# Gate logits of the first chunk on POOL and ACT, wider feature instructions, other homes for the key masks, an uneven last tile and a seeded planner, in a fused attention and feed-forward kernel

## The chip, the cores and the metric

One core of one Trainium2 chip runs the whole program. The metric is device time in microseconds (us), the median of several executions; lower is better. Single executions of one kernel here mostly lie within 0.3% of each other. The chip names five engines: TensorE (PE), VectorE (DVE), ScalarE (ACT), GpSimd (POOL) and SyncE (SP, used to issue DMAs).

## The reference, cut to what matters

The input x is 2048 tokens by 512 features, bf16. A per-token gate `g` mixes an attention branch `a` and a gated feed-forward branch `b`:

```python
g = sigmoid((x * gate_w).sum(-1, keepdims=True))     # one number per token
a = A_ref(x, wq, wk, wv, wo, beta)                   # 32 heads of 16, four segments ("chunks") of 512 tokens
b = B_ref(x, W_gate, W_up, W_down)                   # relu(x Wg) * (x Wu), then W_down
return g * a + (1 - g) * b
# A_ref, per chunk: softmax attention inside the chunk, mixed with a memory
#   a_mem = phi(q) M / (phi(q) z + 1e-6);  phi(t) = t + 1 if t > 0 else exp(t)
#   M and z are then updated with phi(k) and v of this chunk
```

Of the kernel before, what the change touches and what calls it, by code (L numbers as in the profile page):

```python
# [1 line left out]

# [53 lines left out]
class Op:  # L56
    __slots__ = ("engs", "eng", "fns", "occs", "lat", "reads", "writes", "name", "dma", "nbytes", "mode", "ep", "role",
                 "after", "preds", "stream", "idx", "start", "end", "done", "cidx", "gate")

    def __init__(self, alts, reads=(), writes=(), name="", lat=0.0, dma=False, nbytes=0, mode="f", ep=None, role=None):  # L60
# [15 lines left out]
        self.gate = None  # L76
        self.stream = self.idx = self.start = self.end = None
# [9 lines left out]
class Sched:  # L87
# [3 lines left out]
    def __init__(self, ndma=16, nbanks=4):  # L91
# [11 lines left out]
        self.dma_end = {}  # L103
        self.dma_busy = 0.0
# [131 lines left out]
    def _waits(self, e, deps):  # L236
        for st, idx in sorted(deps.items(), key=lambda kv: (kv[0] == e, kv[0])):
            if idx <= 0 or self.know[e][st] >= idx:
                continue
            self.prog[e].append(("wait", st, 16 * idx if st.startswith("dma") else idx))  # L240
            kn = self.know[e]
            for k2, v2 in self.snap[st][idx].items():
                if v2 > kn[k2]:
                    kn[k2] = v2
            kn[st] = max(kn[st], idx)

    def place(self, op, e, start):
# [18 lines left out]
        if op.dma:  # L266
# [4 lines left out]
            self.cnt[st] += 1  # L271
            inc = 16
# [20 lines left out]

    def _choose(self, e):
# [17 lines left out]
        if rdy:  # L312
            best = min(rdy, key=lambda h: (h[0], h[1]))
# [26 lines left out]
    def emit(self, block):  # L340
        sec = {"pe": block.tensor, "act": block.scalar, "dve": block.vector, "pool": block.gpsimd, "sp": block.sync}
        for e in self.ENGS:
            def body(engobj, prog=self.prog[e], e=e):
                for item in prog:
                    if item[0] == "wait":
                        engobj.wait_ge(self.sem[item[1]], item[2])
                    else:
                        _, op, st, inc = item
                        op.fns[e](engobj).then_inc(self.sem[st], inc)
# [3 lines left out]
def plan(S, D, F):  # L353
# [11 lines left out]
        ("gwc", [128, KT], BF16), ("braw", [128, 32], BF16), ("eb", [128, 32], F32), ("romgh", [128, 32], F32), ("epsv", [128, 32], F32),  # L365
        ("gexp", [128, NT], F32), ("omg", [128, NT], F32), ("gexpT", [128, NT * 4], F32), ("c2g", [128, 2, 4, 32], F32), ("gwb", [128, 512], BF16), ("gl", [128, NT], F32),
        ("rden", [128, 32], F32), ("rdg", [128, 32], F32), ("rdm", [128, 128], F32), ("pm8", [128, 8], F32), ("pm", [128, 2], F32), ("ident", [128, 128], BF16), ("g4", [4, 128], BF16),
# [3 lines left out]
def build_kernel(nc, A_x, A_wq, A_wk, A_wv, A_wo, A_beta, W_g, W_u, W_d, gate_w, out):  # L371
# [5 lines left out]
    sc = Sched()  # L377
# [14 lines left out]
def program(sc, nc, T, PL, PA, A_x, A_wq, A_wk, A_wv, A_wo, A_beta, W_g, W_u, W_d, gate_w, out, NSEG, KT, NF, NT, EPS, SCALE):  # L392
# [34 lines left out]
    for i, eng in enumerate(("sp", "act", "sp", "act")):  # L427
# [4 lines left out]
    load("act", ["g4"], V.g4[:], gate_w.rearrange("(kt p) -> kt p", p=128), 1 << 12)  # L432
# [17 lines left out]
    load("sp", ["gwb"], V.gwb[:], gate_w.partition_broadcast(128), 1 << 17)  # L450
# [58 lines left out]
    xps.append(warm(8, 128, 1, 0))  # L509
# [13 lines left out]
    ep_w = Epoch()  # L523
    gw_pe = pe(lambda e: e.matmul(A(ep_w)[:, 0:KT], lhsT=V.g4[:, :], rhs=V.ident[0:KT, 0:KT], start=True, stop=True), 60, reads=["g4", "ident"], name="gwT", ep=ep_w, role="w")
    gw_act = act(lambda e: e.activation(V.gwc[:], A(ep_w)[:, 0:KT], ACT.Copy), 180, writes=["gwc"], name="gwc", ep=ep_w, role="r")
    gw_pe.after = 9000.0
    gexpT_r = {}
    gq = {"pe": [], "act": [], "dve": [], "flex": [], "sp": []}
    for c in range(NSEG):
        t0, t1 = 4 * c, 4 * c + 4  # L530
        gx = V.gexp[:, t0:t1]
        if c == 0:
            ep_g = Epoch()

            def f_gmm(e):
                for t in range(4):
                    for kt in range(KT):
                        ins = e.matmul(A(ep_g)[:, t:t + 1], lhsT=V.xT[:, kt, t * 128:(t + 1) * 128], rhs=V.gwc[:, kt:kt + 1], start=(kt == 0), stop=(kt == KT - 1))
                return ins
            gq["pe"].append(pe(f_gmm, 4 * KT * 26.0, reads=xt(0) + ["gwc"], name="gmm", ep=ep_g, role="w"))  # L540
            gq["act"].append(act(lambda e, gx=gx: e.activation(gx, A(ep_g)[:, 0:4], ACT.Exp), 190, writes=[f"gexp{c}"], name="gexp", ep=ep_g, role="r"))
        else:
# [6 lines left out]
            gq["act"].append(act(lambda e, t0=t0, t1=t1, gx=gx: e.activation(gx, V.gl[:, t0:t1], ACT.Exp), 215, reads=[f"gl{t}" for t in range(t0, t1)], writes=[f"gexp{c}"], name="gexp"))  # L549
# [4 lines left out]
        for a in range(4):  # L554
            for jj in range(4):
                dst = V.gexpT[32 * jj:32 * jj + 32, :].rearrange("q (t a) -> q t a", a=4)[:, t0:t1, a]
# [367 lines left out]
```

## The kernel before: what the change and the argument touch

The kernel is not written as a fixed stream. It lists operations with their reads, writes and an estimated cost. A planner places them: on each engine it always takes, from the heads of several queues with priorities, the operation that its own cost estimates say is ready. The result is one fixed instruction order for each engine, with semaphore waits. So **a change of one operation or one estimate can reorder everything after it**, and the hardware then runs that order strictly, engine by engine.

```python
    def _choose(self, e):                      # pick the next operation of engine e
        ...
        rdy = [h for h in heads if h[1] <= now + 20.0]
        if rdy:
            best = min(rdy, key=lambda h: (h[0], h[1]))    # priority, then ready time
            return best[2], best[1]
        ...
```

Gate of chunk 0 on PE, the rest on DVE, then 16 small copies per chunk that spread the gate over partitions:

```python
gw_pe = pe(... matmul of gate_w and an identity ..., name="gwT")        # gate_w into a column
gw_act = act(... V.gwc <- PSUM ...)
if c == 0:
    def f_gmm(e):                              # 16 one-column matmuls
        for t in range(4):
            for kt in range(KT):
                ins = e.matmul(A(ep_g)[:, t:t + 1], lhsT=V.xT[:, kt, ...], rhs=V.gwc[:, kt:kt + 1], ...)
    gq["act"].append(act(... V.gexp <- exp(PSUM) ...))
...                                            # other chunks: DVE multiplies and sums
for a in range(4):                             # "gate copies": 32x4 elements each
    for jj in range(4):
        gq["flex"].append(... ("dve", tensor_copy, 150), ("act", Copy, 215) ..., name="gexpT")
```

Masked keys, the feature map phi in halves of 512 columns, and a score "quad": four row-tiled matmuls into one PSUM area, whose exp on ACT (1.88 us each, 80 of them) must end before the next quad may write there.

```python
km = lambda e: e.tensor_scalar(V.kp[:, ks, :], V.kT[:, G, :], V.pm[:, p:p + 1], None, ALU.mult)
alts = [("dve", km, 390)] + ([("pool", km, 680)] if s else [])
...
acts.append(act(... V.phiq[:, G, :] <- exp(qT) ..., name=f"qexp{s}_{G}"))
sbs.append(dve(... V.ttmp <- max(qT, 0) + 1 ..., name=f"qts{s}_{G}"))
sbs.append(dve(... V.phiq <- min(V.phiq, V.ttmp) ..., name=f"qphi{s}_{G}"))
...
pes.append(pe(fq, ..., writes=[f"bankL{b}" for b in range(4)], name=f"quad{s}_{tag}", mode="r"))
acts.append(act(... V.E <- exp(SCALE * PL) ..., reads=bankL, name=f"exp{s}_{tag}"))
```

Small constants at the start: `eb = exp(beta)` on ACT, then `romgh = eb + 1` and `epsv = 1e-6 * romgh` on DVE. The last output tile is computed as two pieces of 256 columns, so that the final eviction and store are small.

The softmax here doesn't subtract the row's maximum and nothing guards it: scores larger than these inputs give would overflow.

## Time and profile before

| | before |
|---|---|
| time, median of 3 (later 6 with the pairing runs) | 273.62 us (273.89) |
| span of the profiled execution | 272.4 us |
| busy PE / DVE / ACT / POOL | 264.6 / 206.2 / 196.0 / 120.9 us |

The head of the profile page of the kernel before: busy time with its share of the span and the number of instructions, then PE's busy share in 40 slices of the span (9 is 90% or more).

```profile
PE 264.6 (97%) x2126; PEld 115.8 (43%) x2161; DVE 206.2 (76%) x411; ACT 196.0 (72%) x194; POOL 120.9 (44%) x168
...
PE   8999999999998999999999999999999999999996
```

PE is busy all the way but for the first and last slices and one in the middle. A busy PE is not yet a PE at its peak, because the ends of matmuls are modelled. So a second reading was made: the distance from the **start** of one matmul to the start of the next, for each pair of shapes. Its median is what I call the *spacing*. An excess over it is a *stall*. In this trace a 512-column matmul follows another after 216 ns, 128 columns after 59 ns; the Trainium skill ("TensorE: Matmul & The Clock Gate", section "Wait — 56ns, not 53.3ns?") gives N/2.4 GHz plus about 2.5 ns when warm, 215.7 ns for 512, and this trace agrees. For 128 columns the same formula gives 55.8 ns, and the trace has 59, 3 ns more. A full-array matmul before a score quad takes 312 ns, 96 more. The skill's "TensorEngine Tiling (Array Packing)", section "Key Properties", says that a change of tiling mode drains the engine. The drain itself is not seen in the trace, but the longer spacing fits it and puts a number to it.

Put to the whole order, the spacings explain the time up to the cold start and few stalls. The largest stall is told by the list of waits of PE (two of its lines; the first is the head of the program):

```profile
PE psL L492 <- PEq L909: 0.8, 1, 0.8
PE psA L652 <- DVE phiq L603: 0.8, 1, 0.8
```

L652 are the denominators of the memory read, L603 the last step of phi(q). The timeline just before shows what L603 stood behind on DVE (columns: start us, us, engine, line, operation, shapes):

```profile
83.14 0.69 DVE L781 TENSOR_SCALAR rl<-psA 128x512 bf16<-128x512 f32 x1 [0.32 <-PE psA L772]
83.86 2.11 DVE L557 COPY gexpT<-gexp 32x4 f32<-32x4 f32 x7
84.14 1.23 POOL L699 TENSOR_SCALAR_AFFINE_SELECT E<-E 128x512 bf16<-128x512 bf16 x2 [0.32 <-ACT E L696]
86.01 0.42 DVE L603 TENSOR_TENSOR phiq<-phiq,ttmp 128x512 bf16<-128x512 bf16 x1
```

and PE in the same stretch:

```profile
85.09 0.60 PE L811 MATMUL psA<-wd,hT 128*128 128x512 bf16 x2
86.49 0.59 PE L652 MATMUL psA<-Mbd,phiq 128*128 128x8 bf16 x16 [0.79 <-DVE phiq L603]
```

Seven gate copies of four columns each hold DVE for 2.11 us, and PE stands for 0.79 us by the profile, 0.93 us by the spacings. The planner had put 150 ns on such a copy; on DVE they took 240 ns on average. The groups (count, then busy us and mean ns, then idle time before) that the change bears on:

```profile
L608 POOL TENSOR_SCALAR kp<-kT,pm 128x512 bf16<-128x512 bf16 x16 | 27.3, 1708 | 1.4 <-PE psL L691 0.8 <-DVE kT L605 0.4
L608 DVE TENSOR_SCALAR kp<-kT,pm 128x512 bf16<-128x512 bf16 x16 | 6.8, 430 | 1.3 <-PE psL L691 1.3
L558 ACT ACTIVATE gexpT<-gexp 32x4 f32<-32x4 f32 x40 | 8.3, 206 | 1.0
L557 DVE COPY gexpT<-gexp 32x4 f32<-32x4 f32 x24 | 5.8, 240 | 0.7
L538 PE MATMUL psA<-gwc,xT 128*128 128x1 bf16 x16 | 0.6, 164 | 0.0
```

The masks on POOL (L608) were planned at 680 ns and took 1708. The start, where PE waits for neither of the first two quads (`eb` comes when the load of beta, `braw`, has landed):

```profile
10.68 0.23 ACT L514 ACTIVATE eb<-braw 128x32 f32<-128x32 bf16 x1 [4.42 <-DMA braw<-in_A_beta_dram]
13.55 0.40 PE L691 MATMUL psL<-qT,kp 32*128 32x512 bf16 x4
14.05 1.86 ACT L696 ACTIVATE E<-psL 128x2048 bf16<-128x2048 f32 x1
```

The end of the program, with the two 256-column pieces:

```profile
269.28 0.60 PE L804 MATMUL psA<-wo,oT 128*128 128x256 bf16 x4
269.92 0.47 ACT L821 ACTIVATE osb<-psA,omg 128x256 bf16<-128x256 f32 x1 [1.43 <-PE psA L804]
```

### The profile page before, as it was taken

The numbers are of one execution on the slowest core, as the hardware profiler recorded it, in microseconds if no ns is written. First come the engines' busy times: TensorE is split into PE (matmuls) and PEld (weight loads), VectorE is DVE, ScalarE is ACT, GpSimd is POOL, SyncE is SP. The second block draws the span as 40 slices with busy tenths as digits, with TensorE's granted clock in tenths as the row PEclk, the third lists the DMA queues.
The fourth block names the chain that finished last, engine by engine and source line by source line (L and its number), as shares of the span: only waits on it lengthen the run. The fifth ranks groups of instructions, "written<-read, shape, count | busy, mean of one in ns | idle before, by whom it ended". The sixth has DMA issues, their size and how long they took to land.

```text
span 272.4 us, 5341 instructions
## 1 busy us (share of the span) xinstructions
PE 264.6 (97%) x2126; PEld 115.8 (43%) x2161; DVE 206.2 (76%) x411; ACT 196.0 (72%) x194; POOL 120.9 (44%) x168
## 2 busy tenths in 40 slices
PE   8999999999998999999999999999999999999996
PEld 5444434443443443443435343434344343444445
DVE  4789999999999989998987958885956274957200
ACT  3279898898798778888878977977887676952122
POOL 5023397879495374934364743243433333320000
PEclk9999999999999999999999999999999999999999
DMA  7999934301200234100113110100120000000011
GB/s 231 272 361 207 282 60 92 45 23 39 59 2 1 61 77 99 39 22 0 23 21 76 41 58 22 40 1 0 22 45 17 28 30 23 0 2 0 0 41 39
DMA packets 31025, 17.01 MB, mean 62 GB/s; under 512 B 20760, under 2 KB 31000, under 8 KB 31000
## 3 DMA queue, kind: packets, MB, share of 16 engines
q1 hardware_dynamic: 30416, 16.14, 23.9%
q10 hardware_dynamic: 584, 0.53, 0.7%
q8 instruction: 17, 0.28, 0.4%
q14 instruction: 8, 0.07, 0.1%
HBM read 9.84 MB, written 2.10 MB: 44 GB/s over the span
## 4 chain that ended last, share of the span: by engine, by line
PE 92%; DVE 4%; issue 2%; DMA 1%; ACT 0%
PE psA L772 36%; PE psA L811 16%; PE psA L592 10%; PE psL L691 9%; PE psA L717 7%; PE psA L590 5%; PE psA L804 4%; DVE gexpT L557 1%; PE psA L665 1%; DMA hT<-in_A_x_dram 1%; PE psA L636 1%; PE psL L500 1%; PE psA L652 1%; DVE qT L599 0%; PE psL L492 0%
## 5 line engine op out<-in xcount | busy, mean ns | idle before, releaser
L696 ACT ACTIVATE E<-psL 128x2048 bf16<-128x2048 f32 x80 | 150.0, 1875 | 33.6 <-PE psL L691 32.4
L699 POOL TENSOR_SCALAR_AFFINE_SELECT E<-E 128x512 bf16<-128x512 bf16 x128 | 83.4, 671 | 116.6 <-ACT E L696 111.9
L772 PE MATMUL psA<-xT,wu 128*128 128x512 bf16 x216 | 58.5, 380 | 0.7 <-issue 0.3
L772 PE MATMUL psA<-xT,wg 128*128 128x512 bf16 x213 | 57.2, 380 | 1.1 <-issue 0.8
L811 PE MATMUL psA<-wd,hT 128*128 128x512 bf16 (+1 forms) x230 | 53.0, 367 | 0.8 <-issue 0.6
L783 DVE TENSOR_TENSOR hT<-psA,rl 128x512 bf16<-128x512 f32 x56 | 38.0, 680 | 10.5 <-PE psA L772 10.2
L811 PEld LDWEIGHTS psA<-wd,hT 128*128 128x128 bf16 x238 | 21.6, 98 | 24.0 <-issue 3.8
L691 PE MATMUL psL<-qT,kp 32*128 32x384 bf16 (+3 forms) x512 | 31.7, 301 | 0.0
L780 ACT ACTIVATE rl<-psA 128x512 bf16<-128x512 f32 x34 | 20.3, 597 | 15.2 <-PE psA L772 11.2
L772 PEld LDWEIGHTS psA<-xT,wg 128*128 128x128 bf16 x224 | 20.2, 98 | 25.0 <-issue 3.1
L772 PEld LDWEIGHTS psA<-xT,wu 128*128 128x128 bf16 x224 | 20.3, 98 | 24.8 <-issue 2.0
L608 POOL TENSOR_SCALAR kp<-kT,pm 128x512 bf16<-128x512 bf16 x16 | 27.3, 1708 | 1.4 <-PE psL L691 0.8
L722 DVE STREAM_TRANSPOSE Tn<-psA 128x512 f32<-128x512 f32 x32 | 21.0, 692 | 6.7 <-PE psA L717 6.7
L691 PEld LDWEIGHTS psL<-qT,kp 32*128 32x128 bf16 x512 | 8.9, 92 | 33.5 <-ACT E L696 15.7
L717 PE MATMUL psA<-E,vaug 128*17 128x256 bf16 (+3 forms) x512 | 20.2, 300 | 0.0
L820 DVE TENSOR_SCALAR osb<-psA,omg 128x512 bf16<-128x512 f32 x10 | 7.4, 744 | 14.1 <-PE psA L811 14.1
L781 DVE TENSOR_SCALAR rl<-psA 128x512 bf16<-128x512 f32 x22 | 15.1, 687 | 3.8 <-PE psA L772 3.5
L592 PE MATMUL psA<-xT,wq 128*128 128x512 bf16 x62 | 16.3, 384 | 0.2 <-issue 0.2
L804 PE MATMUL psA<-wo,oT 128*128 128x512 bf16 (+1 forms) x67 | 16.2, 366 | 0.2 <-DVE oTt L736 0.2
L592 PE MATMUL psA<-xT,wk 128*128 128x512 bf16 x60 | 15.8, 380 | 0.3 <-issue 0.2
L590 PE MATMUL psA<-wv,xT 128*128 128x512 bf16 x63 | 15.5, 380 | 0.1
L717 PEld LDWEIGHTS psA<-E,vaug 128*17 128x17 bf16 x512 | 10.7, 90 | 9.6 <-issue 2.7
(74 smaller groups left out, 236.9 us busy)
## 6 DMA issues: line engine op xcount, KB each, us to landing
out_dram<-osb SPq DMA_DIRECT2D x15, 128.0 KB, 1.7
wg<-in_B_W_gate_dram SPq DMA_DIRECT2D x8, 224.0 KB, 6.1
wu<-in_B_W_up_dram SPq DMA_DIRECT2D x8, 224.0 KB, 6.5
wd<-in_B_W_down_dram SPq DMA_DIRECT2D x1, 1792.0 KB
osb<-in_A_x_dram SPq DMA_DIRECT2D x12, 128.0 KB, 2.2
wk<-in_A_wk_dram SPq DMA_DIRECT2D x4, 128.0 KB, 4.0
wv<-in_A_wv_dram SPq DMA_DIRECT2D x4, 128.0 KB, 3.6
wo<-in_A_wo_dram SPq DMA_DIRECT2D x1, 512.0 KB, 5.4
```

Of the source, the lines that this page charges most:

```text
L590: ins = e.matmul(A(ep)[:, :], lhsT=V.xT[:, kt, tok + col * 128:tok + (col + 1) * 128], rhs=w[:, kt, :], start=(kt == 0), stop=(kt == KT - 1))
L592: ins = e.matmul(A(ep)[:, :], lhsT=w[:, kt, col * 128:(col + 1) * 128], rhs=V.xT[:, kt, tok:tok + 512], start=(kt == 0), stop=(kt == KT - 1))
L608: km = lambda e, G=G, p=p, ks=ks: e.tensor_scalar(V.kp[:, ks, :], V.kT[:, G, :], V.pm[:, p:p + 1], None, ALU.mult)
L691: ins = q.matmul(PL[:, jj, o:o + w], lhsT=V.kp[32 * jj:32 * jj + 32, kslot(s, n), 128 * j:128 * j + 128], rhs=V.qT[32 * jj:32 * jj + 32, q ...
L696: acts.append(act(lambda a, e=e: a.activation(V.E[:, e, :, :], PL[:, :, :], ACT.Exp, scale=SCALE), t_act(2048), reads=[f"bankL{b}" for b i ...
L699: pools.append(pool(lambda g, ap=ap: g.affine_select(out=ap, in_=ap, compare_op=ALU.is_ge, fill=0.0, base=0, pattern=[[0, 4], [1, 128]], c ...
L717: ins = q.matmul(A(ep)[32 * jj:32 * jj + 17, c:512], lhsT=V.vaug[:, s % 2, j, 8 * G + 2 * jj + p, :], rhs=V.E[:, e, jj, o:o + w], start=(j ...
L722: ds.append(dve(lambda e, p=p, ep=eps[p]: e.transpose(V.Tn[:, p, :], A(ep)[:, :]), t_dve(512), writes=[f"Tn{p}"], name=f"tr{s}_{G}_{p}", e ...
L772: ins = e.matmul(A(ep)[:, :], lhsT=w[:, kt, f * 128:(f + 1) * 128], rhs=V.xT[:, kt, c * 512:(c + 1) * 512], start=(kt == 0), stop=(kt == K ...
L783: evs.append(dve(lambda e, ep=eu, r=r, hs=hs: e.tensor_tensor(V.hT[:, hs, :], A(ep)[:, :], V.rl[:, r, :], ALU.mult), t_dve(512), reads=[f" ...
L804: ins = e.matmul(A(ep)[:, 0:c1 - c0], lhsT=V.oT[:, o0 + G, i * 128:(i + 1) * 128], rhs=V.wo[:, G, c0:c1], start=st_ and G == 0, stop=sp_ a ...
L811: ins = e.matmul(A(ep)[:, 0:c1 - c0], lhsT=V.hT[:, slots[f], i * 128:(i + 1) * 128], rhs=V.wd[:, f, c0:c1], start=st_ and f == f0, stop=sp ...
```

## The change

Its intent: take the gate of chunk 0 off PE, the bottleneck; halve the number of phi instructions; move the slow key masks off POOL; make the last eviction smaller; correct several of the planner's cost estimates; and let seeded random offsets of up to 400 ns decide among operations that are ready at equal priority, so that many orders can be tried.

```diff
     def _choose(self, e):
-            best = min(rdy, key=lambda h: (h[0], h[1]))
+            best = min(rdy, key=lambda h: (h[0], h[1] + self.jitter(h[2])))   # random() * 400 per operation, seed 59
@@ loads
-    load("act", ["g4"], V.g4[:], gate_w.rearrange("(kt p) -> kt p", p=128), 1 << 12)
+    load("act", ["gwb"], V.gwb[:], gate_w.partition_broadcast(128), 1 << 17)
-    load("sp", ["gwb"], V.gwb[:], gate_w.partition_broadcast(128), 1 << 17)          # was late, on SP
@@ gate of chunk 0 (gwT, gwc and the 16 gate matmuls removed)
+            for t in range(4):
+                gq["pool"].append(pool(... Tn[t % 2] <- hT[t] * gwb ..., 1250, name=f"gml{t}"))
+                gq["act"].append(act(... Copy of Tn[t % 2], accum_out=V.gl[:, t:t + 1] ..., name=f"gad{t}"))
@@ gate copies: contiguous destination, cost 150 -> 200 on DVE
@@ phi: for odd G, one instruction of 128x1024 for groups G-1 and G
-    alts = [("dve", km, 390)] + ([("pool", km, 680)] if s else [])
+    alts = [("dve", km, 420)] + ([("act", ka, 720)] if s else [])
@@ last tile
-    for c0, c1 in (((0, 512),) if t < NT - 1 else ((0, 256), (256, 512))):
+    for c0, c1 in (((0, 512),) if t < NT - 1 else ((0, 384), (384, 512))):
@@ one warm-up matmul fewer; estimates of three DVE operations raised; the first x tiles swap queues
```

More of the change, by code (lines that the diff above doesn't have):

```diff
@@ L1 @@
 import contextlib
+import random
 import numpy as np
@@ L57 @@
     __slots__ = ("engs", "eng", "fns", "occs", "lat", "reads", "writes", "name", "dma", "nbytes", "mode", "ep", "role",
-                 "after", "preds", "stream", "idx", "start", "end", "done", "cidx", "gate")
+                 "after", "preds", "stream", "idx", "start", "end", "done", "cidx", "gate", "nd")
     def __init__(self, alts, reads=(), writes=(), name="", lat=0.0, dma=False, nbytes=0, mode="f", ep=None, role=None):
@@ L76, in __init__ @@
         self.gate = None
+        self.nd = 1
         self.stream = self.idx = self.start = self.end = None
@@ L89, with __init__ @@
     CAPS = {"ffn": 3, "proj": 2, "mid": 2, "out": 2}
-    def __init__(self, ndma=16, nbanks=4):
+    def __init__(self, ndma=16, nbanks=4, seed=0):
+        self.rng = random.Random(seed)
+        self.jit = {}
         self.bank_ep = [None] * nbanks
@@ L103, in __init__ @@
         self.dma_end = {}
+        self.semval = {}
         self.dma_busy = 0.0
@@ L239, in _waits @@
                 continue
-            self.prog[e].append(("wait", st, 16 * idx if st.startswith("dma") else idx))
+            self.prog[e].append(("wait", st, self.semval[st, idx] if st.startswith("dma") else idx))
             kn = self.know[e]
@@ L271, in place @@
             self.cnt[st] += 1
+            self.semval[st, self.cnt[st]] = self.semval.get((st, self.cnt[st] - 1), 0) + 16 * op.nd
             inc = 16
@@ L292, with jitter @@
     TOL = {"pe": 400.0, "act": 150.0, "dve": 250.0, "pool": 300.0, "sp": 300.0}
+    def jitter(self, op):
+        j = self.jit.get(op.cidx)
+        if j is None:
+            j = self.jit[op.cidx] = self.rng.random() * 400.0
+        return j
     def _choose(self, e):
@@ L348, in body @@
                         _, op, st, inc = item
-                        op.fns[e](engobj).then_inc(self.sem[st], inc)
+                        res = op.fns[e](engobj)
+                        for r in (res if op.nd > 1 else [res]):
+                            r.then_inc(self.sem[st], inc)
             sec[e](body)
@@ L364, in plan @@
         ("Mbd", [128, 4, 136], F32), ("Mbd16", [128, 4, 136], BF16), ("mumask", [128, 2, 136], BF16), ("mutmp", [128, 2, 136], F32),
-        ("gwc", [128, KT], BF16), ("braw", [128, 32], BF16), ("eb", [128, 32], F32), ("romgh", [128, 32], F32), ("epsv", [128, 32], F32),
+        ("braw", [128, 32], BF16), ("eb", [128, 32], F32), ("romgh", [128, 32], F32), ("epsv", [128, 32], F32),
         ("gexp", [128, NT], F32), ("omg", [128, NT], F32), ("gexpT", [128, NT * 4], F32), ("c2g", [128, 2, 4, 32], F32), ("gwb", [128, 512], BF16), ("gl", [128, NT], F32),
-        ("rden", [128, 32], F32), ("rdg", [128, 32], F32), ("rdm", [128, 128], F32), ("pm8", [128, 8], F32), ("pm", [128, 2], F32), ("ident", [128, 128], BF16), ("g4", [4, 128], BF16),
+        ("rden", [128, 32], F32), ("rdg", [128, 32], F32), ("rdm", [128, 128], F32), ("pm8", [128, 8], F32), ("pm", [128, 2], F32), ("ident", [128, 128], BF16),
     ]
@@ L376, in build_kernel @@
     EPS, SCALE = 1e-6, 16 ** -0.5
-    sc = Sched()
+    sc = Sched(seed=59)
     T = {}
@@ L426, in program @@
     x0 = A_x[0, 0:512, :].rearrange("(i p) d -> p i d", p=128)
-    for i, eng in enumerate(("sp", "act", "sp", "act")):
+    for i, eng in enumerate(("act", "sp", "act", "sp")):
         load(eng, [f"hT{i}"], V.hT[:, i, :], x0[:, i, :], 1 << 17)
@@ L508, in program @@
             xcs.append(act(lambda e, d=dst, s_=srcp: e.activation(d, s_, ACT.Copy), t_act(512), reads=[f"bankL{i}"], writes=[f"xT0_{i}"], name=f"xc{i}"))
-    xps.append(warm(8, 128, 1, 0))
+    xps.append(warm(7, 128, 1, 0))
     sc.queue(0, xps)
@@ L521, in program @@
     sc.queue(1, [t for t in cst if t.eng == "dve"])
-    ep_w = Epoch()
-    gw_pe = pe(lambda e: e.matmul(A(ep_w)[:, 0:KT], lhsT=V.g4[:, :], rhs=V.ident[0:KT, 0:KT], start=True, stop=True), 60, reads=["g4", "ident"], name="gwT", ep=ep_w, role="w")
-    gw_act = act(lambda e: e.activation(V.gwc[:], A(ep_w)[:, 0:KT], ACT.Copy), 180, writes=["gwc"], name="gwc", ep=ep_w, role="r")
-    gw_pe.after = 9000.0
     gexpT_r = {}
-    gq = {"pe": [], "act": [], "dve": [], "flex": [], "sp": []}
+    gq = {"pe": [], "act": [], "dve": [], "flex": [], "pool": [], "sp": []}
     for c in range(NSEG):
@@ L532, in program @@
         if c == 0:
-            ep_g = Epoch()
-            def f_gmm(e):
-                for t in range(4):
-                    for kt in range(KT):
-                        ins = e.matmul(A(ep_g)[:, t:t + 1], lhsT=V.xT[:, kt, t * 128:(t + 1) * 128], rhs=V.gwc[:, kt:kt + 1], start=(kt == 0), stop=(kt == KT - 1))
-                return ins
-            gq["pe"].append(pe(f_gmm, 4 * KT * 26.0, reads=xt(0) + ["gwc"], name="gmm", ep=ep_g, role="w"))
-            gq["act"].append(act(lambda e, gx=gx: e.activation(gx, A(ep_g)[:, 0:4], ACT.Exp), 190, writes=[f"gexp{c}"], name="gexp", ep=ep_g, role="r"))
+            for t in range(4):
+                gq["pool"].append(pool(lambda e, t=t: e.tensor_tensor(V.Tn[:, t % 2, :], V.hT[:, t, :], V.gwb[:], ALU.mult), 1250, reads=[f"hT{t}", "gwb"], writes=[f"Tn{t % 2}"], name=f"gml{t}"))
+                gq["act"].append(act(lambda e, t=t: e.activation(V.Tn[:, t % 2, :], V.Tn[:, t % 2, :], ACT.Copy, accum_out=V.gl[:, t:t + 1]), t_act(512, False) + 100, reads=[f"Tn{t % 2}"], writes=[f"Tn{t % 2}", f"gl{t}"], name=f"gad{t}"))
         else:
@@ L548, in program @@
                                      t_dve(512) + 70, reads=["osb2_0", "osb2_1", "gwb"], writes=["osb2_0", "osb2_1", f"gl{t}"], name=f"gate{t}"))
-            gq["act"].append(act(lambda e, t0=t0, t1=t1, gx=gx: e.activation(gx, V.gl[:, t0:t1], ACT.Exp), 215, reads=[f"gl{t}" for t in range(t0, t1)], writes=[f"gexp{c}"], name="gexp"))
+        gq["act"].append(act(lambda e, t0=t0, t1=t1, gx=gx: e.activation(gx, V.gl[:, t0:t1], ACT.Exp), 215, reads=[f"gl{t}" for t in range(t0, t1)], writes=[f"gexp{c}"], name="gexp"))
         om = V.omg[:, t0:t1]
@@ L555, in program @@
             for jj in range(4):
-                dst = V.gexpT[32 * jj:32 * jj + 32, :].rearrange("q (t a) -> q t a", a=4)[:, t0:t1, a]
-                gq["flex"].append(sc.add(Op([("dve", lambda e, a=a, dst=dst, t0=t0, t1=t1: e.tensor_copy(dst, V.gexp[32 * a:32 * a + 32, t0:t1]), 150),
+                dst = V.gexpT[32 * jj:32 * jj + 32, 16 * c + 4 * a:16 * c + 4 * a + 4]
+                gq["flex"].append(sc.add(Op([("dve", lambda e, a=a, dst=dst, t0=t0, t1=t1: e.tensor_copy(dst, V.gexp[32 * a:32 * a + 32, t0:t1]), 200),
                                              ("act", lambda e, a=a, dst=dst, t0=t0, t1=t1: e.activation(dst, V.gexp[32 * a:32 * a + 32, t0:t1], ACT.Copy), 215)],
@@ L565, in c2g @@
                    t_dve(128), reads=["eb", f"gexp{s}"], writes=[f"c2g{s % 2}"], name=f"c2g{s}")
-    sc.queue(3, [gw_pe] + gq["pe"])
-    sc.queue(1, [gw_act] + gq["act"])
+    sc.queue(1, gq["act"])
+    sc.queue(1, gq["pool"])
     sc.queue(1, gq["dve"])
@@ L576, in qslot, with phi @@
         return (s % 2) * 4 + G
+    def phi(s, px, G, dst, dn, src, slot, rd, acts, sbs):
+        xv, pv = src[:, slot:slot + 2, :], dst[:, G - 1:G + 1, :]
+        wr = [f"{dn}{G - 1}", f"{dn}{G}"]
+        acts.append(act(lambda e: e.activation(pv, xv, ACT.Exp), t_act(1024, False), reads=rd, writes=wr, name=f"{px}exp{s}_{G}"))
+        sbs.append(dve(lambda e: e.tensor_scalar(V.ttmp[:, :, :], xv, 0.0, 1.0, ALU.max, ALU.add), t_dve(1024, 4) + 50, reads=rd, writes=["ttmp"], name=f"{px}ts{s}_{G}"))
+        sbs.append(dve(lambda e: e.tensor_tensor(pv, pv, V.ttmp[:, :, :], ALU.min), t_dve(1024, 2) + 120, reads=wr + ["ttmp"], writes=wr, name=f"{px}phi{s}_{G}"))
     def proj(s):
@@ L599, in proj @@
             evs.append(dve(lambda e, ep=ep, qs=qs: e.tensor_copy(V.qT[:, qs, :], A(ep)[:, :]), t_dve(512), writes=[f"qT{qs}"], name=f"qcp{s}_{G}", ep=ep, role="r"))
-            if s > 0:
-                acts.append(act(lambda e, qs=qs, G=G: e.activation(V.phiq[:, G, :], V.qT[:, qs, :], ACT.Exp), t_act(512, False), reads=[f"qT{qs}"], writes=[f"phiq{G}"], name=f"qexp{s}_{G}"))
-                sbs.append(dve(lambda e, qs=qs, G=G: e.tensor_scalar(V.ttmp[:, G % 2, :], V.qT[:, qs, :], 0.0, 1.0, ALU.max, ALU.add), t_dve(512, 4), reads=[f"qT{qs}"], writes=[f"ttmp{G % 2}"], name=f"qts{s}_{G}"))
-                sbs.append(dve(lambda e, G=G: e.tensor_tensor(V.phiq[:, G, :], V.phiq[:, G, :], V.ttmp[:, G % 2, :], ALU.min), t_dve(512, 2), reads=[f"phiq{G}", f"ttmp{G % 2}"], writes=[f"phiq{G}"], name=f"qphi{s}_{G}"))
+            if s > 0 and G % 2:
+                phi(s, "q", G, V.phiq, "phiq", V.qT, qs - 1, [f"qT{qs - 1}", f"qT{qs}"], acts, sbs)
             ep = pj(V.wk, G, "k", "wk")
@@ L608, in proj @@
                 km = lambda e, G=G, p=p, ks=ks: e.tensor_scalar(V.kp[:, ks, :], V.kT[:, G, :], V.pm[:, p:p + 1], None, ALU.mult)
-                alts = [("dve", km, 390)] + ([("pool", km, 680)] if s else [])
-                evs.append(sc.add(Op(alts, reads=[f"kT{G}", "pm"], writes=[f"kp{ks}"], name=f"kmask{s}_{G}_{p}")))
-            if s < NSEG - 1:
-                acts.append(act(lambda e, G=G: e.activation(V.ek[:, G, :], V.kT[:, G, :], ACT.Exp), t_act(512, False), reads=[f"kT{G}"], writes=[f"ek{G}"], name=f"kexp{s}_{G}"))
-                sbs.append(dve(lambda e, G=G: e.tensor_scalar(V.ttmp[:, G % 2, :], V.kT[:, G, :], 0.0, 1.0, ALU.max, ALU.add), t_dve(512, 4), reads=[f"kT{G}"], writes=[f"ttmp{G % 2}"], name=f"kts{s}_{G}"))
-                sbs.append(dve(lambda e, G=G: e.tensor_tensor(V.ek[:, G, :], V.ek[:, G, :], V.ttmp[:, G % 2, :], ALU.min), t_dve(512, 2), reads=[f"ek{G}", f"ttmp{G % 2}"], writes=[f"ek{G}"], name=f"kphi{s}_{G}"))
-                sps.append(dma("sp", lambda e, G=G: e.dma_start_transpose(V.phik[:, :, G * 128:(G + 1) * 128], V.ek[:, G, :]), 1 << 17, occ=1280.0, reads=[f"ek{G}"], writes=[f"phik{G}"], name=f"kT2{s}_{G}"))
+                ka = lambda e, G=G, p=p, ks=ks: e.activation(V.kp[:, ks, :], V.kT[:, G, :], ACT.Copy, scale=V.pm[:, p:p + 1])
+                evs.append(sc.add(Op([("dve", km, 420)] + ([("act", ka, 720)] if s else []), reads=[f"kT{G}", "pm"], writes=[f"kp{ks}"], name=f"kmask{s}_{G}_{p}")))
+            if s < NSEG - 1 and G % 2:
+                phi(s, "k", G, V.ek, "ek", V.kT, G - 1, [f"kT{G - 1}", f"kT{G}"], acts, sbs)
+                for g in (G - 1, G):
+                    sps.append(dma("sp", lambda e, g=g: e.dma_start_transpose(V.phik[:, :, g * 128:(g + 1) * 128], V.ek[:, g, :]), 1 << 17, occ=1280.0, reads=[f"ek{g}"], writes=[f"phik{g}"], name=f"kT2{s}_{g}"))
         for tt in range(4):
@@ L728, in flush @@
             ds.append(dve(lambda e: e.reciprocal(rv, Tv[:, :, :, 16]), 345, reads=["Tn0", "Tn1"], writes=["rden"], name=f"rden{s}_{G}"))
-            ds.append(dve(lambda e: e.tensor_tensor(gv, rv, V.gexpT[:, 16 * s:16 * s + 16].unsqueeze(1).to_broadcast([128, 2, 16]), ALU.mult), 264, reads=["rden"] + gexpT_r[s], writes=["rdg"], name=f"rdg{s}_{G}"))
+            ge = V.gexpT[:, 16 * s:16 * s + 16].rearrange("q (a t) -> q t a", t=4).unsqueeze(1).to_broadcast([128, 2, 4, 4])
+            ds.append(dve(lambda e: e.tensor_tensor(gv.rearrange("q p (t a) -> q p t a", a=4), rv.rearrange("q p (t a) -> q p t a", a=4), ge, ALU.mult), 310, reads=["rden"] + gexpT_r[s], writes=["rdg"], name=f"rdg{s}_{G}"))
             av = V.adT[:, :].rearrange("q (c p e) -> q p c e", p=2, e=16)
-            ds.append(dve(lambda e: e.tensor_tensor(av, Tv[:, :, :, 0:16], gv.unsqueeze(3).to_broadcast([128, 2, 16, 16]), ALU.mult), 806, reads=["Tn0", "Tn1", "rdg"], writes=["adT"], name=f"ad{s}_{G}"))
+            ds.append(dve(lambda e: e.tensor_tensor(av, Tv[:, :, :, 0:16], gv.unsqueeze(3).to_broadcast([128, 2, 16, 16]), ALU.mult), 870, reads=["Tn0", "Tn1", "rdg"], writes=["adT"], name=f"ad{s}_{G}"))
             os_ = (s % 2) * 4 + G
@@ L736, in flush @@
                 ds.append(dve(lambda e: e.transpose(V.oTt[:, :], V.adT[:, :]), t_dve(512), reads=["adT"], writes=["oTt"], name=f"bt{s}_{G}"))
-                ds.append(dve(lambda e: e.tensor_tensor(V.oT[:, os_, :], V.oTt[:, :], V.amemT[:, G, :], ALU.add), t_dve(512, 2), reads=["oTt"] + [f"amemT{i}" for i in range(4)], writes=[f"oT{os_}"], name=f"oa{s}_{G}"))
+                ds.append(dve(lambda e: e.tensor_tensor(V.oT[:, os_, :], V.oTt[:, :], V.amemT[:, G, :], ALU.add), 540, reads=["oTt"] + [f"amemT{i}" for i in range(4)], writes=[f"oT{os_}"], name=f"oa{s}_{G}"))
             return pair
@@ L818, in outp @@
                 om = V.omg[:, t:t + 1]
-                res = [f"osb{r}_0", f"osb{r}_1"] if w == 512 else [f"osb{r}_{c0 // 256}"]
+                res = [f"osb{r}_0", f"osb{r}_1"] if w == 512 else [f"osb{r}_{c0 // 384}"]
                 evs.append(sc.add(Op([("dve", lambda e, ep=ep, r=r, om=om, c0=c0, c1=c1: e.tensor_scalar(V.osb[:, r, c0:c1], A(ep)[:, 0:c1 - c0], om, None, ALU.mult), t_dve(w)),
@@ L880, in program @@
     sc.queue(1, Q["poolmu"])
-    sc.queue(1, Q["spk"])
+    sc.queue(0, [t for t in Q["spk"] if t.nd > 1])
+    sc.queue(1, [t for t in Q["spk"] if t.nd == 1])
     sc.queue(1, Q["spa"])
@@ L888, in program @@
         if sc.cnt[f"dma{i}"]:
-            sc.prog["sp"].append(("wait", f"dma{i}", 16 * sc.cnt[f"dma{i}"]))
+            sc.prog["sp"].append(("wait", f"dma{i}", sc.semval[f"dma{i}", sc.cnt[f"dma{i}"]]))
 def bass_gated_mix__memory_aug_infini_attn__glu_gated_reglu__prompt_kernel(
```

## The prediction

> **What bounds the kernel now.** TensorE, by issue. The page gives PE 264.6 us busy of a 272.4 us span (97%; DVE 76%, ACT 72%, POOL 44%), and the chain that ended last is PE for 92%. Since PE ends are modelled, I measured start to start in the timeline: 512-column matmuls follow each other every 216 ns, 128-column ones every 59 ns, four row-tiled score matmuls issue together, a full-array matmul before a score quad takes 312 ns (96 more than normal), score-to-full 317, 147 or 200 ns by width. The Trainium skill, "TensorE: Matmul & The Clock Gate", gives N/2.4 GHz plus about 2.5 ns start to start when warm: 215.7 ns for 512; the trace agrees (216). Applying this table of spacings to the whole order of before gives 264.4 us from first to last matmul start; the trace has 268.8. The rest is the cold start (427 and 107 ns spacings, and the first x tile's DMA, until 6.3 us) and one real stall: 0.82 us at 85.3 us, where the denominators (L652) wait for DVE's phi(q).
>
> **What the change does.**
> 1. PE: the 17 gate matmuls of chunk 0 go (0.17 + 0.55 us and one array switch); a warm-up matmul goes, but the first projection waits for ACT's last transpose copy anyway (ends 6.26, PE starts 6.32): no gain. The last tile as 384+128 costs PE some 0.2 us (36 x 109 ns becomes 18 x 162 + 18 x 60). Order: 80 switches into score mode rather than 81, 65 out of it rather than 67. The same spacing table on the new order gives 263.9: 0.6 us less.
> 2. Tail: the last eviction has 128 columns, not 256 (0.47 us; by the 512-column one at 0.69, about 0.36) and half the store: 0.1 to 0.2 us.
> 3. POOL loses 16 key masks of 1.71 us (27.3 us) and gains four multiplies (est. 1.3 us each). They become 7 on DVE, 9 on ACT (est. 0.7).
> 4. DVE: 48 phi instructions become 24 double ones, saving mostly fixed cost; 8 more relus (0.69), 17 fewer 0.24 us copies. Net about -3 us of 206. ACT: net about +8 of 196 (four gate sums, nine masks, 17 copies, eight fewer relus at 0.60).
>
> Items 3 and 4 are off the critical path; they count only through stalls. The 0.82 us stall should mostly go. New risk at the start: ACT now runs four gate sums, a 1024-wide exp and copies before the first score exp, fed by an earlier gate-weight load and four POOL multiplies. Counting from a landing near 7 us, the first exp ends near 16.9 us (14.05+1.86 before), when PE wants the second quad. I allow 0.5 us of stall there and 0.3 elsewhere.
>
> **Sum.** 273.6 - 0.6 - 0.8 - 0.15 + 0.8 = about 272.8; the seeded order probably is tighter than I can see, so 272.6, range 271.4 to 274.0. Faster by over 2%: 0.01; within 2%: 0.97; slower: 0.02. Over 2% (5.5 us) isn't to be had, PE's issue being the floor.
>
> **What would show it.** PE still about 97%, the spacings the same; no wait of L652's successor on phi; POOL near 97 us; ACT near 204, DVE near 203; first score exp ending 16.5 to 17.5 us; the last store issued sooner after PE's end.
>
> **What would make it wrong.** POOL multiplies slower than 1.5 us, or the gate weights landing late, so that the first exps and PE slip by 1 us or more; ACT's added work delaying score exps (PE waiting on ACT at quads); DVE, 95% busy from 20 to 120 us, made later by its new relus.

## The result, and the profile after

The changed kernel took 272.93 us (median of 6, 272.25 to 273.37); the kernel before in the same rounds and the first ones 273.89. The ratio is 0.9965, 95% interval 0.9949 to 0.9981. Ratios in this document are those of the record, taken over the fast runs of the same rounds, so they aren't quite the ratio of the medians quoted. The gain is real, about 0.96 us (0.35% of 273.9), and within 2%.

The head of the page of the changed kernel:

```profile
PE 263.0 (97%) x2108; PEld 115.1 (42%) x2143; DVE 204.8 (76%) x382; ACT 203.7 (75%) x210; POOL 99.5 (37%) x156
...
PE   8989999999999999999999999999999999999996
```

The dip in the middle is gone and one has come in the third slice. PE's waits say which (the 0.8 us at the head of the program, seen before too, is left out):

```profile
PE psL L698 <- DVE kp L616: 0.5, 1, 0.5
PE psL L698 <- ACT E L703: 0.3, 1, 0.3
```

L698 is the score quad. By the spacings these are 0.57 us before the first quad and 0.40 us before the second. No wait for phi(q) is left. PE at the start:

```profile
9.82 3.62 PE L602 MATMUL psA<-xT,wk 128*128 128x512 bf16 x15
13.94 0.39 PE L698 MATMUL psL<-qT,kp 32*128 32x512 bf16 x4 [0.51 <-DVE kp L616]
14.27 3.20 PE L600 MATMUL psA<-wv,xT 128*128 128x512 bf16 x14
17.80 0.40 PE L698 MATMUL psL<-qT,kp 32*128 32x384 bf16 x8 [0.34 <-ACT E L703]
```

What stood in front of them. POOL's multiplies wait for the gate weights, which landed at 8.36 us; ACT takes the gate sums and `eb` in a fixed order, `eb` after the second sum; DVE waits for `eb`:

```profile
8.51 4.48 POOL L543 TENSOR_TENSOR Tn<-hT,gwb 128x512 f32<-128x512 bf16 x4 [4.01 <-DMA gwb<-in_gate_w_dram]
```

```profile
11.43 0.21 ACT L527 ACTIVATE eb<-braw 128x32 f32<-128x32 bf16 x1
13.78 0.20 ACT L552 ACTIVATE gexp<-gl 128x4 f32<-128x4 f32 x1
14.01 0.89 ACT L561 ACTIVATE gexpT<-gexp 32x4 f32<-32x4 f32 x4
14.93 1.06 ACT L584 ACTIVATE ek<-kT 128x1024 bf16<-128x1024 bf16 x1
15.89 1.86 ACT L703 ACTIVATE E<-psL 128x2048 bf16<-128x2048 f32 x1
```

```profile
11.67 0.24 DVE L528 TENSOR_SCALAR romgh<-eb 128x32 f32<-128x32 f32 x1 [0.96 <-ACT eb L527]
11.84 0.68 DVE L613 CAST kT<-psA 128x512 bf16<-128x512 f32 x1
12.44 0.59 DVE L529 TENSOR_SCALAR epsv<-romgh 128x32 f32<-128x32 f32 x1
12.95 0.68 DVE L613 CAST kT<-psA 128x512 bf16<-128x512 f32 x1
13.55 0.60 DVE L616 TENSOR_SCALAR kp<-kT,pm 128x512 bf16<-128x512 bf16 x2
```

Two chains can be read here. One: DVE, free at 10.7 us, stands 0.96 us for the small constant `romgh`, so the copies of k and the first key mask come late, and the mask ends at 13.89, just before the first quad. Not all of that wait is ACT's order: the load of beta landed at 11.12 us in this trace, so `eb`, which ran at 11.43, could have come some 0.3 us sooner and no more. Two: ACT does four gate sums, the gate's exp, four copies and a wide key exp before the first score exp, which so ends at 17.75 (15.91 before), and the second quad waits for it. One more detail: `epsv`, 0.17 us in the kernel before, took 0.59 us and ended at 13.03, just after POOL's fourth multiply at 12.99. The skill's "SBUF — State Buffer", section "Who interferes with whom", says that DVE and GpSimd share a port pair, an exclusive lock held for a whole instruction; this trace agrees with that.

The groups of the changed kernel that answer to those shown of before:

```profile
L561 ACT ACTIVATE gexpT<-gexp 32x4 f32<-32x4 f32 x57 | 11.6, 203 | 1.4
L560 DVE COPY gexpT<-gexp 32x4 f32<-32x4 f32 x7 | 2.4, 344 | 0.2
L616 DVE TENSOR_SCALAR kp<-kT,pm 128x512 bf16<-128x512 bf16 x23 | 9.0, 404 | 0.4 <-PE psL L698 0.2
L617 ACT ACTIVATE kp<-kT,pm 128x512 bf16<-128x512 bf16 x9 | 6.5, 719 | 0.3 <-DVE kT L613 0.2
L543 POOL TENSOR_TENSOR Tn<-hT,gwb 128x512 f32<-128x512 bf16 x4 | 4.5, 1149 | 4.0 <-DMA gwb<-in_gate_w_dram 4.0
```

and its end:

```profile
268.43 0.39 PE L812 MATMUL psA<-wo,oT 128*128 128x128 bf16 x4
268.86 0.37 ACT L829 ACTIVATE osb<-psA,omg 128x128 bf16<-128x128 f32 x1 [0.36 <-PE psA L812]
```

Cutting the two profiled executions at the first score quad and at the start of the last matmul gives:

| stretch, us | before | after | difference |
|---|---|---|---|
| start to first quad | 13.55 | 13.94 | +0.39 |
| first quad to the start of the last matmul | 256.06 | 254.66 | -1.41 |
| start of the last matmul to the end | 2.83 | 2.58 | -0.24 |

In the middle stretch the sum of spacings of the order fell by 0.60 us (254.37 to 253.77; 0.21 us that the table overstates at the gate matmuls is taken off the first), the stalls before two groups of denominators (0.93 and 0.11 us) went, and the one of 0.40 us at the second quad came. That makes -1.24; 0.17 us of the -1.41 isn't assigned to anything. The sums are good to about 0.1 us: some pairs of shapes are rare, and 35 of the 2161 matmuls of before have no record in its trace. The three differences add to -1.26 us, more than the 0.96 between the medians, because the profiled execution of before (274.17 us) was slower than its median.

### The profile page after: what moved, and what is told of

The parts are those of the page before. It is cut to its first block, busy times and chain, and to the rows that moved or that the text cites. A ratio compares the mean times of both kernels' runs of the same rounds, so it can differ in the third digit from the quotient of the medians.

```text
span 271.2 us, 5268 instructions
## 1 busy us (share of the span) xinstructions
PE 263.0 (97%) x2108; PEld 115.1 (42%) x2143; DVE 204.8 (76%) x382; ACT 203.7 (75%) x210; POOL 99.5 (37%) x156
## 4 chain that ended last, share of the span: by engine, by line
PE 88%; ACT 2%; DVE 2%; DMA 2%; issue 2%; POOL 2%; ACTq 1%; DVEq 0%; POOLq 0%
PE psA L780 36%; PE psA L819 17%; PE psL L698 9%; PE psA L602 8%; PE psA L724 7%; PE psA L812 5%; PE psA L600 4%; DMA gwb<-in_gate_w_dram 2%; POOL Tn L543 2%; PE psA L672 1%; PE psA L643 1%; ACT E L703 1%; ACTq L439 1%; DVE osb L828 1%; PE psA L659 0%
## 5 line engine op out<-in xcount | busy, mean ns | idle before, releaser
L706 POOL TENSOR_SCALAR_AFFINE_SELECT E<-E 128x512 bf16<-128x512 bf16 x128 | 85.4, 685 | 139.6 <-ACT E L703 139.5
L780 PE MATMUL psA<-xT,wg 128*128 128x512 bf16 x213 | 58.0, 380 | 1.1 <-issue 0.8
L819 PE MATMUL psA<-wd,hT 128*128 128x512 bf16 (+2 forms) x233 | 53.0, 367 | 0.8 <-issue 0.8
L698 PE MATMUL psL<-qT,kp 32*128 32x384 bf16 (+3 forms) x512 | 31.7, 301 | 0.8 <-DVE kp L616 0.5
L789 DVE TENSOR_SCALAR rl<-psA 128x512 bf16<-128x512 f32 x30 | 20.6, 688 | 4.0 <-PE psA L780 3.0
L698 PEld LDWEIGHTS psL<-qT,kp 32*128 32x128 bf16 x512 | 8.9, 92 | 34.0 <-ACT E L703 14.0
L788 ACT ACTIVATE rl<-psA 128x512 bf16<-128x512 f32 x26 | 15.5, 595 | 10.3 <-PE psA L780 10.2
L829 ACT ACTIVATE osb<-psA,omg 128x512 bf16<-128x512 f32 (+2 forms) x10 | 6.4, 645 | 13.7 <-PE psA L812 13.1
L812 PE MATMUL psA<-wo,oT 128*128 128x512 bf16 (+2 forms) x64 | 15.9, 366 | 0.3 <-issue 0.2
L602 PE MATMUL psA<-xT,wq 128*128 128x512 bf16 x61 | 15.5, 380 | 0.5 <-issue 0.3
L600 PE MATMUL psA<-wv,xT 128*128 128x512 bf16 x61 | 14.7, 380 | 0.4 <-issue 0.3
L724 PEld LDWEIGHTS psA<-E,vaug 128*17 128x17 bf16 x512 | 10.7, 90 | 9.4 <-issue 2.5
L609 DVE CAST qT<-psA 128x512 bf16<-128x512 f32 x16 | 10.7, 676 | 3.4 <-PE psA L602 3.3
```

What stands on the lines that cost most here:

```text
L600: ins = e.matmul(A(ep)[:, :], lhsT=V.xT[:, kt, tok + col * 128:tok + (col + 1) * 128], rhs=w[:, kt, :], start=(kt == 0), stop=(kt == KT - 1))
L602: ins = e.matmul(A(ep)[:, :], lhsT=w[:, kt, col * 128:(col + 1) * 128], rhs=V.xT[:, kt, tok:tok + 512], start=(kt == 0), stop=(kt == KT - 1))
L698: ins = q.matmul(PL[:, jj, o:o + w], lhsT=V.kp[32 * jj:32 * jj + 32, kslot(s, n), 128 * j:128 * j + 128], rhs=V.qT[32 * jj:32 * jj + 32, q ...
L706: pools.append(pool(lambda g, ap=ap: g.affine_select(out=ap, in_=ap, compare_op=ALU.is_ge, fill=0.0, base=0, pattern=[[0, 4], [1, 128]], c ...
L724: ins = q.matmul(A(ep)[32 * jj:32 * jj + 17, c:512], lhsT=V.vaug[:, s % 2, j, 8 * G + 2 * jj + p, :], rhs=V.E[:, e, jj, o:o + w], start=(j ...
L780: ins = e.matmul(A(ep)[:, :], lhsT=w[:, kt, f * 128:(f + 1) * 128], rhs=V.xT[:, kt, c * 512:(c + 1) * 512], start=(kt == 0), stop=(kt == K ...
```

## The experiments

Two techniques. *Pinned*: the kernel's own order was recorded, one operation was moved in it by hand, and the program was built with that fixed order, so that nothing else moves (a pinned build without an edit gave the same instructions and the same waits as the original). *Planned anew*: one part of the change was put in or taken out and the planner ran again, which also reshuffles the rest. All results were correct. "Stalls" are excesses over the spacings, read from each run's own trace.

### 1. Was the stall before the denominators made by the gate copies?

Theory: they stood in front of phi(q) on DVE. Rival: DVE was slowed by POOL's key masks, whatever its order. Pinned, kernel before:

```diff
-dve order: ..., gexpT x7, qphi1_3, ...
+dve order: ..., qphi1_3, gexpT x7, ...
```

> The kernel before with every engine's order pinned to its own, but for one move on VectorE: the last phi(q) minimum of chunk 1 goes ahead of the seven gate-weight copies (2.11 us together) that stood before it. Theory (the 0.82 us PE stall before the chunk-1 denominators came from those copies standing in front): the stall at 85.3 us shrinks to under 0.1 us and the time falls by about 0.8 to 0.9 us. Rival (the stall came from VectorE being slowed by the POOL key masks, so VectorE is late whatever the order): a stall of over 0.4 us stays, and the time falls by less than 0.4 us.

Time 273.57 us against 273.85, ratio 0.9976 with an interval of 0.9933 to 1.0019, so not resolved. The trace decides, for DVE and PE in it:

```profile
83.47 0.41 DVE L636 TENSOR_TENSOR phiq<-phiq,ttmp 128x512 bf16<-128x512 bf16 x1
83.91 2.16 DVE L590 COPY gexpT<-gexp 32x4 f32<-32x4 f32 x7
```

```profile
85.25 0.58 PE L685 MATMUL psA<-Mbd,phiq 128*128 128x8 bf16 x16
```

The denominators now start without a wait (85.25 us, against 86.49). The 0.93 us stall is gone, and the masks were still on POOL: the place of the copies in front of phi(q) made it. But neither theory names POOL's work on E, which held two of the seven copies for 0.77 us; without it, the stall would have been about 0.2 us by the same estimate. No run tests that. And two new stalls of 0.15 us each came at 88.8 and 89.4 us, so from the first quad to the last matmul the gain was 0.65 us (256.06 to 255.42), less than the 0.8 to 0.9 expected.

### 2. What held the first two quads of the changed kernel?

Three pinned edits of the changed kernel, then both together. The copies on POOL were made to wait for each other, one after the other. The expectation of (A) says "behind the first two key masks"; the edit put the constants between the first mask and the second, which serves the first quad as well.

```diff
-dve order: ..., romgh, kcp0_0, epsv, kcp0_1, kmask0_0_0, kmask0_0_1, ...      (A)
+dve order: ..., kcp0_0, kcp0_1, kmask0_0_0, romgh, epsv, kmask0_0_1, ...
-act order: ..., gexp, gexpT x4, kexp0_1, exp0_0A0, ..., gexpT x12 in between   (B)
+act order: ..., gexp, kexp0_1, exp0_0A0, ...;   pool order: gml0..gml3, gexpT x16, ...
```

> The changed kernel, orders pinned, but on VectorE the two small constants that wait for ACT's exp of beta (romgh, epsv) go behind the first two key masks. Theory (the first score quad was late by 0.57 us because VectorE stood waiting for ACT's exp of beta, itself held behind POOL's gate multiplies): the stall before the first quad goes (under 0.1 us); but ACT's chain still starts the first score exp at about 15.9 us, so the wait before the second quad grows from 0.40 to about 0.95 us and the time stays within 0.2 us. Rival (weights landing late after the broadcast gate load held PE up): the stall before the first quad stays.

> The changed kernel, orders pinned, but the 16 small gate copies of chunk 0 are done on POOL instead of ACT. Theory (ACT's chain gate sums, exp, four copies, key exp before the first score exp sets the second quad): the first score exp starts about 0.9 us earlier (15.0 us), the 0.40 us stall before the second quad goes, the 0.57 us stall before the first stays, time down by about 0.4 us. Rival (PE is held at the second quad by something else than ACT's queue): the stall of 0.4 us stays.

> Both edits together on the changed kernel: VectorE's two constants behind the first key masks, and chunk 0's 16 gate copies on POOL. Theory: both stalls at the start (0.57 and 0.40 us) go, none larger than 0.2 us appears, time about 0.9 us under the changed kernel, near 272.0 us, and 1.8 us under the kernel before. Rival (ACT is full until 34 us, so the gain is given back at a later quad): the sum of PE stalls stays near 1 us and the time falls by less than 0.4 us.

| run | stall at first quad | at second quad | first score exp starts | time, ratio to before |
|---|---|---|---|---|
| changed kernel | 0.57 | 0.40 | 15.89 | 272.93, 0.9965 |
| (A) constants behind the mask | none | 0.49 | 15.56 | 273.15, 0.9973 (0.9919 to 1.0026) |
| (B) copies on POOL | 1.18 | none | 15.27 | 272.70, 0.9942 (0.9900 to 0.9984) |
| (A) and (B) | none | 0.04 | 14.57 | 271.92, 0.9917 (0.9874 to 0.9960) |

Each edit took away the stall that it was aimed at and left the other, so the two chains are separate, and late weights are not the cause of the first stall: in (A) the first k weights landed at 8.26 us, much as late as in the changed kernel (8.55), and the stall was gone. Two sizes were missed. In (A) the second stall was to grow to 0.95 us and grew to 0.49 only; in that trace the gate weights landed 0.34 us earlier (8.02) and ACT's chain with them. In (B) the first stall grew to 1.18 instead of staying at 0.57; there the gate weights landed at 8.79 and `eb` ran at 11.86 instead of 11.43. In every trace with the changed kernel's order of ACT and no late beta, `eb` ran 3.07 to 3.08 us after the gate weights landed. So both stalls hang on that landing, which varied from 7.84 to 8.79 us over the traces of this document.

Waits of PE with both edits; no wait for a key mask or a score exp is left:

```profile
PE psL L552 <- PEq L966: 0.8, 1, 0.8
PE psA L650 <- ACT xT L568: 0.2, 1, 0.2
PE psA L650 <- DVE ttmp L633: 0.2, 1, 0.2
PE psA L650 <- DVE rdm L711: 0.2, 1, 0.2
```

The lock showed again: in this run the first key mask on DVE took 0.90 us (0.34 is usual) and ended at 12.88, after POOL's fourth multiply at 12.73. The load of beta landed late here, at 11.84, and `eb` waited for it; with the constants behind the mask that cost PE nothing.

### 3. Parts of the change alone, and taken out

> The kernel before with the gate part of the change alone (gate weights loaded early as a broadcast, four POOL multiplies, four ACT sums, no gate matmuls), planned anew by the old planner. By the measured start-to-start spacings its PE order sums to 0.9 us less than before. Theory (the gate part takes PE work away but pays it back at the start): stalls of 0.4 to 1.5 us in sum stand before the first two score quads, the time lies within 0.6 us of before. Rival (the gate part is the gain of the whole change): no stall over 0.2 us at the start, time 0.9 us or more under before.

273.77 us, ratio 1.0009 (0.9991 to 1.0027): no gain that the runs resolve. Its trace has stalls of 0.51, 0.43 and 0.26 us before the first, second and fourth quad; none before the denominators. The theory held: what PE no longer computes is paid back at the start.

> The changed kernel with the gate part undone (gate matmuls on PE, small gate load, as before), planned anew with the same seed. Its PE order sums to 0.7 us more than the changed kernel's by the spacings. Theory: no stall over 0.2 us at the start; so the time stays within 0.5 us of the changed kernel (0.7 more work, about 1.0 less stall), if the new order brings no stall elsewhere. Rival (the gate part is the whole gain): time 0.7 us or more over the changed kernel, near before.

272.75 us, ratio 0.9966 (0.9951 to 0.9981), the same as the changed kernel's 0.9965. No stall is to be seen after the first matmuls. PE's spacings there sum to 0.8 us more from the first quad on (254.55 against 253.77, the drift that every gate order shows at its gate matmuls, 0.21 us, taken off). The rival, that the gate part is the gain, falls: put in or left out, it nets nothing beyond the intervals, some 0.5 us either way.

> The changed kernel, orders pinned, with the last tile split 256 and 256 again. Theory: from the start of the last matmul to the end 2.8 us instead of 2.6 (the eviction 0.1 us longer, the store twice as large), PE 0.07 us less work, so about 0.15 us longer in all, under what the timed runs resolve. Rival (the split does nothing): the same 2.6 us from the last matmul's start to the end.

Edit: `(0, 256), (256, 512)` again, pinned. From the start of the last matmul to the end 2.83 us, against 2.58; so the uneven split is worth 0.25 us there. It was expected to be told by the trace alone. The time was 273.33 us, ratio 0.9985 (0.9970 to 1.0001), with a first-quad stall of 0.65 us in its trace. That is 0.5 us above the changed kernel's ratio; the profiled executions differ by 0.23 us only, and the intervals overlap.

> The kernel before with only the key masks moved from POOL to VectorE or ACT, planned anew by the old planner. PE spacings sum to the same within 0.1 us. Theory (POOL's masks are off the critical path): POOL busy falls by about 27 us, the time moves only by the stalls that the new order has, within 1 us of before either way. Rival (POOL's masks slow VectorE through a shared path and that costs time): VectorE's 128x512 bf16 minima (phi) fall from 0.54 to 0.58 us to under 0.5 us, no PE stall over 0.2 us is left, and the time falls by 0.7 us or more.

275.19 us, ratio 1.0058 (1.0037 to 1.0080): slower by about 1.6 us by the ratio (1.2 by the medians; one run of four took 276.76), where theory said within 1 us and the rival said faster. POOL's busy time fell to 93.4 us from 120.9, as expected, and PE's spacing sum was the same within 0.1 us. The stall of 0.93 us of before is down to 0.2, but there is a new one of 1.70 us at 172.4 us, again before denominators, again behind gate copies on DVE:

```profile
PE psA L653 <- DVE phiq L603: 1.6, 1, 1.6
```

```profile
168.71 1.79 DVE L557 COPY gexpT<-gexp 32x4 f32<-32x4 f32 x5
170.87 0.42 DVE L603 TENSOR_TENSOR phiq<-phiq,ttmp 128x512 bf16<-128x512 bf16 x1
171.60 0.78 DVE L603 TENSOR_TENSOR phiq<-phiq,ttmp 128x512 bf16<-128x512 bf16 x1
```

The rival fell too: the phi minima for q took 471 ns on average instead of 576, but those for k 589 instead of 539. That the key masks slow DVE enough to cost time isn't shown. POOL's work on E does slow it here: two of the five copies took 617 and 560 ns and the last phi(q) 782 instead of 424, all while such an instruction of POOL ran. That is about 1.2 of the 1.70 us, an estimate from these durations that no run tests.

### 4. What the seed is worth

Edit for the first run: `self.rng.random() * 400.0` becomes `0.0`. For the second: the offsets and seed 59 put into the planner of the kernel before, nothing else.

> The changed kernel with the planner's random offsets set to zero, all else kept. Its PE order has the same sum of spacings as the changed kernel (263.9 us). Theory (the seed only moves stalls about): time within 0.7 us of the changed kernel, any difference being seen as PE stalls in the trace. Rival (the seed found an order that carries the gain): time over 1 us more than the changed kernel, at or above before.

274.59 us, ratio 1.0029 (1.0014 to 1.0044): slower than the changed kernel by about 1.7 us and slower than the kernel before. The PE order's spacing sum is the same as the seeded one's within 0.1 us. The difference is stalls: 0.35, 0.44 and 0.70 us at the second and third quad and at 88.9 us, all waits for ACT, and some smaller ones about 83 to 86 us.

```profile
PE psL L698 <- ACT E L703: 1.4, 4, 0.6
```

The rival held, not my theory of 0.7 us at most.

> The kernel before with nothing but the planner's random offsets added, seed 59 as in the changed kernel. PE spacings sum to 0.1 us less. Theory (a seed is a draw of stalls and is good only with the operations it was picked for): the stalls fall elsewhere, the time lies within 1.5 us of before, likelier above it than below. Rival (the seed in itself is the gain): the time falls by 0.7 us or more.

273.26 us, ratio 0.9976 (0.9963 to 0.9989): 0.65 us faster than before. In its trace the 0.93 us stall at the denominators of chunk 1 is gone; stalls of 0.18, 0.37 and 0.13 us elsewhere are left. It came out at the good end of what the theory allowed and at the rival's line (0.65 us by the ratio, 0.73 by the medians, against 0.7), so it decides between them only in part. A random order alone gives the old operations about half to two thirds of the gain of the whole change: 0.24%, against 0.35% in the first job and 0.47% for the changed kernel in this one (section 5). Only the one seed was tried.

### 5. The best version once more

> The changed kernel again, to stand beside the version with the fixed start on the same chip. Expected by every theory: 0.995 to 0.998 of the time before; stalls of 0.4 to 1.6 us in sum before the first two score quads, varying with the landing of the gate weights.

> The version with both start edits again. Theory (the start stalls of the changed kernel are worth about 1 us): 0.991 to 0.994 of the time before and 0.8 to 1.2 us under the changed kernel of this job, no stall over 0.2 us at the first two quads. Rival (its first result was a lucky start of the DMAs): within 0.4 us of the changed kernel.

On the same chip: the changed kernel 272.58 us, ratio 0.9953 (0.9942 to 0.9965); with the fixed start 272.19 us, ratio 0.9947 (0.9926 to 0.9968). Five of the six runs of the fixed start lie from 271.52 to 272.30 us, the sixth at 273.88 without a trace to say why. The trace again had no stall at the first two quads, and the changed kernel's had 0.26 and 0.41 us. So the mechanism is confirmed and the size is not: 0.4 us between the medians, less than the 0.8 to 1.2 expected and inside the rival's "within 0.4 us", and the intervals overlap. The two profiled executions differ by 1.07 us (272.59 and 271.52), but they are one pair. Together with its first result (271.92 us) the fixed start is the fastest version measured, faster than before by clearly resolved amounts in both jobs and likely, not certainly, faster than the changed kernel.

## Why the prediction was right, point by point

- **The bound and the class.** PE's issue was the floor, and the spacings were the same before and after; nothing moved the time by over 2%. Right.
- **Spacing sum, 0.6 us less.** Confirmed at 0.60 us from the first quad on. Its own item for the last tile, "some 0.2 us" more, was an error of arithmetic: 36 x 109 ns against 18 x 162 + 18 x 60 ns is 0.07 us.
- **The tail, 0.1 to 0.2 us.** Measured 0.24 in the two profiles and 0.25 by the pinned split. The eviction took 0.37 us (0.36 estimated).
- **The 0.82 us stall should mostly go.** It went. The cause was named only as DVE's lateness; experiment 1 shows the place of the gate copies, not the key masks. The reason for its going is a new order, and in part luck: with the seed alone on the old kernel it went as well, and so it did in the changed kernel without the seed, but the new order of the masks alone brought one of 1.70 us.
- **0.5 us of stall at the start and 0.3 elsewhere.** The sum came out near by luck, because two errors cancel: there were 0.97 us at the start, nearly twice what was allowed, and nothing elsewhere. Two terms were mis-sized. The gate weights were put at "a landing near 7 us" and landed at 8.36, while the POOL multiplies, feared slow, took 1.15 us (1.3 estimated). And the first exp, foreseen to end near 16.9 us, ended at 17.75. The stall at the *first* quad was not foreseen at all: it came through `eb`, a small exp that nobody needed soon, standing in front of DVE's first copies of k. Its load landed at 11.12 us, and ACT's order put it some 0.3 us later, behind a gate sum.
- **Busy times.** ACT 204 expected, 203.7 measured; POOL 97, 99.5; DVE 203, 204.8. They moved as foreseen and, as foreseen, mattered through stalls only.
- **"The seeded order probably is tighter than I can see".** This was a guess that took 0.2 us off the sum, and it points to what the prediction had not seen: of the parts taken out here, the seed is the largest. Without it the same operations are slower than the kernel before.

So where did the gain come from? Less PE work (0.6 us) is paid back by the start stalls (0.97 us); the gate part nets nothing in either direction. What is left is the tail (0.24 us) and an order without the 0.93 us stall and without others like it. The wider phi instructions, the corrected estimates and the loads that swapped queues were not tested by themselves; what they add to that order is open.

## What to carry to other kernels

When a planner fixes the order of each engine and one engine is full, the operations decide the floor, but the order decides the last per cent: here one draw of random offsets moved the time by 1.7 us and the whole list of intended changes by less. Look for tiny instructions in front of something that the full engine will need: four-column copies stood in front of stalls of 0.9 us (shown by a pinned move) and 1.7 us (read from the timeline), and a wait for one exp of 32 columns made 0.6 us. Look also at the single durations of such instructions, not at the mean: a copy of 165 ns took 560 when POOL was at work. Work taken off the bottleneck early in a program must not put a chain of DMA, POOL and ACT in front of that engine's first inputs; pin the order and move one instruction to see what such a chain costs.

## What the Trainium skill lacked or had wrong

- "TensorEngine Tiling (Array Packing)", section "Key Properties", says that a change of tiling mode drains TensorE, without a number. Here a full-array matmul of 512 columns before a row-tiled quad takes 312 ns instead of 216, so 96 ns per change into that mode, in some 80 places.
- "ScalarE: Activation LUTs" doesn't tell that an ACTIVATE with an accumulated sum is followed by an instruction of its own: each of the four gate sums here was a 0.63 us ACTIVATE and a 0.19 us ACTIVATION_READ_ACCUMULATOR.
- "DMA: Bandwidth & Descriptors" has, as far as I found, no figure for a small row broadcast to 128 partitions at the start of a program. Here the 128 KB one landed 5.2 to 6.1 us after its issue at 2.7 us, and in the trace of the changed kernel the first k weights behind it landed at 8.55 us instead of 7.05. Over all traces the first k weights landed at 7.83 to 8.58 us with the early broadcast (nine traces) and at 6.83 to 7.31 without (five), though the broadcast was never the only difference.
- "SBUF — State Buffer", section "Who interferes with whom": nothing wrong; a DVE mask held to 0.90 us until POOL's multiply ended agrees with it. What it lacks is how much the lock costs small instructions: a copy of 32x4 f32 on DVE took 159 to 168 ns by itself and up to 561 in the kernel before when an instruction of POOL had started just before it.
